# Linear attention and gated GLU: K features beside the Q projection, Q features beside the GLU stages, x turned by VectorE, output weights split in GLU 0

## The chip, the cores and the metric

The kernel runs on one core of one Trainium2 chip. The metric is the device time of one execution in microseconds; a version's time is the median of its runs. A profile is one execution, whose own time is given beside the time of the profiled span.

## What is computed

The input x is 2048 tokens of 1024 features, in fp32. After a layer norm it goes two ways, and the results are joined:

```python
xn = layernorm(x)
qkv = (xn @ wqkv)                      # q, k, v: 32 heads of 32
pq, pk = q @ w_phi, k @ w_phi          # per head
phi = concat(softmax(p), softmax(-p))  # 64 features, for q and k
kv, z = phi_k^T @ v, sum(phi_k)        # per head, over all tokens
s = (phi_q @ kv / (phi_q @ z + 1e-6)) @ wo
h = sigmoid(xn @ w_gate) * (xn @ w_up) # 3584 wide
out = x + s * silu(h @ w_down)
```

## The kernel before

All large products go to TensorE as f32r pairs: `split` (L121) casts a tile to f32r on ScalarE (L123) and has VectorE subtract that from the tile (L124), and `mm3` (L126) adds three matmuls, high by high, high by low, low by high. On top of that each large product is done with seven block products instead of eight; the blocks are named B11, T2, T3, B21, T1, T4 and B22. The T blocks and B22 of an operand are sums and differences of four quarters, made by GpSimd.

Tokens are done in two chunks of 1024 (`c` = 0, 1; eight tiles of 128 each). TensorE runs through six stages: the projections V, K, Q of chunk 0 (each seven blocks of four token tiles), GLU 0 (gate and up products of chunk 0: 28 units of seven blocks, twelve matmuls each), the same two for chunk 1, then down (`dsteps`), and the output stage (`attend` and wo). w_phi is folded into the K and Q weights, so that a projection's result is already the argument of the softmax.

Around these products stand tasks that other engines do:

- `k_task` (L429): loads k and v of a token tile and of one half of the heads (`hb`), takes the softmax features (`features`, L401: two reductions and two subtractions on VectorE, the exponential on ScalarE, a sum and a reciprocal on VectorE), scales them, splits features and v, adds them into `zacc`. Its small matmuls (`kv_products`, L454) come with the next task. There are 32, and after each 16 three finals (`kv_sum`, `kv_blocks`, `z_broadcast`).
- `q_features` (L565): the same features for q, kept in DRAM (`e_d`, `r_d`), for chunk 0 only. `q_task` (L573) in down loads them, or makes the features itself for chunk 1, then divides by the denominators and stores them into `f_d`.
- `x_task` (L501): loads a tile of chunk 1's x, norms it, turns it by eight TensorE transposes into PSUM (`transpose`, L183), copies it out on ScalarE and stores the block operands into `xo_d`. `load_operand` (L205) fetches them at the end of GLU 0 in two halves, through slots 53 and 54, and splits them into x0 to x6.
- `o_sums` (L256) and `wd_sums` (L546): the sums for wo's and w_down's blocks, into DRAM. `wo_prep` (L617) loads a piece of wo through a ring of two half slots and splits it, in down and at the turn into the output stage.

What sets the order: instructions are emitted in the order of the program, and a scheduler that simulates the engines places them; each engine then runs its own list in order. `background` (L768) takes the next task of a queue and lets it be issued after an anchor, an evacuation of the block at hand. Before, queue `bg` holds 16 q features and 8 x tasks, then K tasks and finals, and `bg2` the sums. GLU 0 takes one task per unit at T2 (L859), chunk 1's projections take the first eight K tasks (L793), GLU 1 a task every six blocks and a sum every ten (L862 to L866), and down the `q_task`s (L938). On-chip memory is cut into slots: 0 to 27 for the x operands, 28 to 35 for split weights (a ring of eight), 36 to 38 `p`, 39 to 42 `fa`, 43 to 46 `fb`, 47 to 54 `fc`. Loads and stores are issued by SyncE, in one list.

```python
            if c and len(bg) > 2 * (TT + 3) - EARLY and i not in (B11, B21):
                background(last_evac[0])
...
            if len(bg) > 2 * (TT + 3) and i == T2 and m > 7:
                background(v.ins)
```

## Time and profile before

| | us |
|---|---|
| median of three runs (lowest, highest) | 2428.53 (2424.84, 2431.23) |
| the profiled execution's own time | 2428.67 |
| its span | 2426.7 |
| TensorE busy in the span | 2364.4 |
| VectorE busy | 1752.7 |
| ScalarE busy | 999.1 |
| GpSimd busy | 982.7 |

The stages in the span lie at about 0 to 300 (chunk 0's projections), to 842 (GLU 0), to 1078 (chunk 1's projections), to 1654 (GLU 1), to 2207 (down) and to the end (output). PE is TensorE's matmuls, PEld its weight loads, DVE VectorE, ACT ScalarE, POOL GpSimd. A table by stretches gives the bounds of a stretch, its length, the busy time of the five with their instructions, the clock granted to TensorE as a share of full speed, the busy share of the DMA engines and GB/s. A row by line gives line, engine, operation, what it writes and reads, the shapes and the count, then busy time and the mean of one, then the idle time of its engine before it and what ended that. Matmul records overlap, so their lengths don't add up to time.

### The profile page before, as it was taken

To read this page: it belongs to the slowest core of one execution; us is meant where nothing else is said; L and a number is where in the kernel's file an instruction comes from. 1 tells how busy PE (TensorE), PEld (TensorE's weight loads), DVE (VectorE), ACT (ScalarE), POOL (GpSimd) and SP (SyncE) were. 2 spreads that over 40 slices of the span, in tenths; PEclk is the share of its full clock that TensorE was granted. 3 is DMA by queue.
4 is the path that set the end of the run, shared out by engine and by line. 5 is a ranking of instruction groups with operands and counts; after the bars stand their busy time and mean duration, and the time that the engine had idled before them with its cause. 6 is when DMAs were issued, how large, how long until landed. Compare 5 with 4: busy or idle time off the path is not lost.

```text
span 2426.7 us, 31652 instructions
## 1 busy us (share of the span) xinstructions
PE 2364.4 (97%) x10792; PEld 1957.0 (81%) x10792; DVE 1752.7 (72%) x2325; ACT 999.1 (41%) x1495; POOL 982.7 (40%) x638
## 2 busy tenths in 40 slices
PE   6999999999999999999999999999999999999998
PEld 5888888888888888888878888788888788877786
DVE  7533567777676688648858888746888998878775
ACT  6432244445444444324433444423443334355342
POOL 4530145665666410003454444442333344313555
PEclk9999999999999999999999999999999999999999
DMA  7874567777776764557888888796677767775564
GB/s 275 276 258 164 173 235 257 266 264 252 261 262 249 255 246 164 191 178 247 286 294 286 276 302 287 250 349 214 209 231 225 244 213 222 236 259 180 192 196 161
DMA packets 245329, 581.59 MB, mean 240 GB/s; under 512 B 31920, under 2 KB 48304, under 8 KB 240560
## 3 DMA queue, kind: packets, MB, share of 16 engines
q1 hardware_dynamic: 245168, 579.58, 69.8%
q8 instruction: 85, 1.39, 0.2%
q14 instruction: 76, 0.62, 0.1%
HBM read 353.76 MB, written 225.71 MB: 239 GB/s over the span
## 4 chain that ended last, share of the span: by engine, by line
PE 68%; DVE 10%; DMA 9%; issue 6%; POOL 4%; ACT 2%; SPq 1%; POOLq 0%; ACTq 0%; DVEq 0%
PE bank L128 22%; PE bank L129 22%; PE bank L130 22%; DVE x L124 2%; DVE w L124 2%; DMA fa<-w_down 1%; DMA w<-ws_d 1%; PE bank L454 1%; DMA fb<-w_down 1%; POOL fc L1020 1%; DMA fc<-wo 1%; DMA f_d<-fc 1%; POOL fc L1019 1%; DMA wf_d<-x 1%; ACT x L123 1%
## 5 line engine op out<-in xcount | busy, mean ns | idle before, releaser
L128 PE MATMUL bank<-x,w 128*128 128x512 f32 x2352 | 911.1, 391 | 9.5 <-DVE fb L835 2.9
L129 PE MATMUL bank<-x,w 128*128 128x512 f32 x2352 | 917.1, 390 | 2.3 <-DVE x L124 2.2
L130 PE MATMUL bank<-x,w 128*128 128x512 f32 x2352 | 904.5, 389 | 0.4 <-DVE w L124 0.4
L124 DVE TENSOR_TENSOR w<-fa,w 128x512 fp32r<-128x512 f32 (+1 forms) x444 | 436.7, 989 | 140.5 <-ACT w L123 139.0
L123 ACT CAST w<-fa 128x512 fp32r<-128x512 f32 (+1 forms) x444 | 307.9, 698 | 547.4 <-PE bank L129 337.5
L128 PEld LDWEIGHTS bank<-x,w 128*128 128x128 f32 x2352 | 441.3, 188 | 105.9 <-DVE fb L835 4.3
L129 PEld LDWEIGHTS bank<-x,w 128*128 128x128 f32 x2352 | 442.1, 188 | 95.0 <-DVE x L124 4.8
L130 PEld LDWEIGHTS bank<-x,w 128*128 128x128 f32 x2352 | 442.0, 188 | 92.5 <-DVE w L124 0.9
L128 PE MATMUL bank<-w,x 128*128 128x512 f32 x708 | 279.3, 395 | 8.0 <-ACT w L123 3.6
L130 PE MATMUL bank<-w,x 128*128 128x512 f32 x708 | 278.1, 394 | 6.1 <-DVE x L124 6.1
L129 PE MATMUL bank<-w,x 128*128 128x512 f32 x708 | 278.3, 393 | 0.0
L128 PEld LDWEIGHTS bank<-w,x 128*128 128x128 f32 x708 | 134.1, 189 | 38.3 <-ACT w L123 4.3
L843 POOL TENSOR_TENSOR fc<-fc 128x512 f32<-128x512 f32 x27 | 42.8, 1586 | 299.6 <-DVE fc L842 295.4
L130 PEld LDWEIGHTS bank<-w,x 128*128 128x128 f32 x708 | 134.3, 190 | 35.2 <-DVE x L124 7.7
L129 PEld LDWEIGHTS bank<-w,x 128*128 128x128 f32 x708 | 134.3, 190 | 27.1
L584 POOL TENSOR_TENSOR fc<-fc 128x1024 f32<-128x1024 f32 x32 | 81.0, 2530 | 181.2 <-ACT fc L419 122.0
L843 POOL TENSOR_TENSOR fb<-fb,fc 128x512 f32<-128x512 f32 x57 | 91.9, 1613 | 134.9 <-DVE fc L842 125.7
L317 POOL TENSOR_TENSOR fb<-fa 128x512 f32<-128x512 f32 x28 | 36.7, 1309 | 249.2 <-DMA fa<-w_gu 130.3
L124 DVE TENSOR_TENSOR w<-fb,w 128x512 fp32r<-128x512 f32 (+1 forms) x114 | 107.0, 939 | 30.7 <-ACT w L123 23.9
L123 ACT CAST w<-fb 128x512 fp32r<-128x512 f32 (+1 forms) x114 | 71.4, 626 | 135.4 <-PE bank L129 98.7
L842 DVE TENSOR_TENSOR fc<-fc,bank 128x512 f32<-128x512 f32 x84 | 57.2, 681 | 92.6 <-PE bank L130 77.4
L124 DVE TENSOR_TENSOR x<-fa,x 128x512 fp32r<-128x512 f32 x112 | 109.5, 979 | 18.0 <-ACT x L123 18.0
...
## 6 DMA issues: line engine op xcount, KB each, us to landing
ws_d<-w SPq DMA_DIRECT2D x112, 512.0 KB, 3.8
w<-ws_d SPq DMA_DIRECT2D x112, 512.0 KB, 5.6
fa<-w_gu SPq DMA_DIRECT2D x84, 512.0 KB, 4.2
fa<-h_d SPq DMA_DIRECT2D x84, 512.0 KB, 4.4
...
h_d<-fc SPq DMA_DIRECT2D x120, 256.0 KB, 3.6
...
```

The costliest lines, as they stand in the source:

```text
L123: nc.scalar.copy(o[0], src)
L124: return nc.vector.tensor_sub(o[1], src, o[0].bitcast(F32))
L128: nc.tensor.matmul(o, a[0], b[0], start=first, stop=False, **kw)
L129: nc.tensor.matmul(o, a[0], b[1], start=False, stop=False, **kw)
L130: nc.tensor.matmul(o, a[1], b[0], start=False, stop=last, **kw)
L317: nc.gpsimd.tensor_add(s1, a21, a22)
L454: nc.tensor.matmul(kvb[g // 2][:, g % 2 * 256:g % 2 * 256 + 256], v[:, g].rearrange("p a f -> p (a f)"), ph[:, g].rearrange("p a f -> p (a ...
L584: nc.gpsimd.tensor_mul(ez, e, zb)
L842: v = nc.vector.tensor_add(b, u2 if q == 3 else u1, bank)
L843: nc.gpsimd.tensor_mul(g, g, b)
L1019: eng.tensor_mul(y, y, g)
L1020: eng.tensor_add(y, y, xt)
```

## The change

- **x of chunk 1.** `x_task` becomes `x_fetch` and `x_turn`. The first norms the tile and stores it into `xs_d` in four pieces; the second loads it back rearranged and turns it with two VectorE transposes of 32x32 blocks, 128x512 each. Transposes on TensorE and copies on ScalarE are left for chunk 0 alone. The 1024 features stand in another order for this, so the host permutes the rows of the weights and chunk 0's x (`xk`) alike.
- **K.** The eight `k_task`s of chunk 0's first half of heads are queued in its Q projection (five blocks T2 to B22), and what is left of the queue in GLU 0. Chunk 1's projections take eight `wd_sums` at V and K, then five K tasks at Q. GLU 1 takes the other 19 with the finals.
- **q.** 16 `q_features` of chunk 0 stay in GLU 0; the 16 of chunk 1 go to GLU 1. `q_task` in down only loads them.
- **wo.** `o_task` loads, sums and splits a quarter of wo (seven splits) and stores the pairs into `wo_d`; four of them stand at the end of GLU 0's queue. `wo_prep` is one load.
- **Pace.** GLU 0 takes a task at T2 of each unit and also at T4 of the first 14. GLU 1 takes one every four blocks, from one queue in which K and finals, six `wd_sums` and 16 `q_features` are mixed evenly.

The diff, cut to its core:

```diff
...
@@ -182,17 +187,14 @@
-        c, th, u = t // CTT, t % CTT // 4, t % 4
+        th, u = t // 4, t % 4
         for q in range(2):
...
                 nc.tensor.transpose(tp[:, k * P:(k + 1) * P], xt[:, (4 * q + k) * P:(4 * q + k + 1) * P], ident)
-            i = {(0, 0): B11, (1, 0): B21, (1, 1): B22}.get((q, th))
-            if c == 0 and th == 0:
-                operand(c, i, u, tp)
+            if th == 0:
+                operand(0, (B11, B21)[q], u, tp)
             nc.scalar.copy(dst[q], tp)
-            if c and i is not None:
-                operand(c, i, u, dst[q])
...
@@ -253,10 +254,26 @@
-    def o_sums(k, bs):
+    def o_task(k):
+
+        def keep(i, b):
+            o = slots[o_r.next()]
+            split((o[:, 0].bitcast(F32R), o[:, 1].bitcast(F32R)), b)
+            nc.sync.dma_start(wo_d[i, k], o.bitcast(F32).rearrange("p a n -> p (a n)"))
+
+        a11, a12, a21, a22 = bs = halves(52, 53)
         for b, (f, h) in zip(bs, ((0, 0), (0, 1), (1, 0), (1, 1))):
             nc.sync.dma_start(b, wo[(k + 4 * h) * P:(k + 4 * h + 1) * P, f * HB:(f + 1) * HB])
-        w_sums(O, k, *bs)
+        for i, b in ((B11, a11), (B21, a12), (T4, a22)):
+            keep(i, b)
+        nc.gpsimd.tensor_add(a22, a21, a22)
+        nc.gpsimd.tensor_sub(a21, a11, a21)
+        nc.gpsimd.tensor_sub(a11, a22, a11)
+        nc.gpsimd.tensor_sub(a12, a12, a11)
+        for i, b in ((T2, a11), (T3, a21), (T1, a22), (B22, a12)):
+            keep(i, b)
+
+    o_r = Ring((36, 37, 38))
...
@@ -498,13 +519,26 @@
-    def x_task(t):
+    def x_fetch(t):
         xt = x_load(t, 52)
         norm([t], [xt])
+        for n in range(4):
+            nc.sync.dma_start(xs_d[t - CTT, :, :, n].rearrange("q s c -> s q c"),
+                              xt[n * DH:(n + 1) * DH].rearrange("s (q c) -> s q c", q=4))
+
+    def x_turn(t):
         th, u = t % CTT // 4, t % 4
-        transpose(t, xt, halves(53 + th))
+        dst = halves(53 + th)
+        xt = whole(52)
+        nc.sync.dma_start(xt, xs_d[t - CTT].rearrange("q s n c -> (q s) (n c)"))
+        for q in range(2):
+            nc.vector.transpose(dst[q].rearrange("p (k n s) -> p n k s", n=4, s=DH),
+                                xt.rearrange("p (n k d) -> p n k d", n=4, d=DH)[:, :, 4 * q:4 * q + 4])
+            i = {(0, 0): B11, (1, 0): B21, (1, 1): B22}.get((q, th))
+            if i is not None:
+                operand(1, i, u, dst[q])
         if th:
-            x_sums(t // CTT, u, halves(53), halves(54))
+            x_sums(1, u, halves(53), halves(54))
...
@@ -557,14 +591,14 @@
     eqr = Ring((50, 51))
-    qraw = Ring([slots[53][:, 1]])
     zb = whole(54)
-    qf_raw, qf_e = Ring(halves(36)), Ring((37, 38))
+    qf = Ring(((36, 0, 37), (36, 1, 38))), Ring(((43, 0, 44),))
...
-        p, e = qf_raw.next(), whole(qf_e.next())
+        r, a, e = qf[t // CTT].next()
+        p, e = slots[r][:, a], whole(e)
         nc.sync.dma_start(p, qkv_d[Q, t, hb])
...
@@ -572,14 +606,9 @@
         e, ez = whole(eqr.next()), whole(52)
-        if t < CTT:
-            nc.sync.dma_start(e, e_d[t, hb])
-            r = small.tile([P, 32], F32, name=f"r{t}{hb}", tag="r", bufs=2)
-            nc.sync.dma_start(r, r_d[t, hb])
-        else:
-            p = qraw.next()
-            nc.sync.dma_start(p, qkv_d[Q, t, hb])
-            r = features(f"q{t}{hb}", p, e, True)
+        nc.sync.dma_start(e, e_d[t, hb])
+        r = small.tile([P, 32], F32, name=f"r{t}{hb}", tag="r", bufs=2)
+        nc.sync.dma_start(r, r_d[t, hb])
         st = small.tile([P, 5, 16], F32, name=f"sa{t}{hb}", tag="sa", bufs=2)
...
@@ -615,13 +643,7 @@
     def wo_prep(i, k):
-        r = wor.next()
-        if i in (B11, B21, T4):
-            f, h = {B11: (0, 0), B21: (0, 1), T4: (1, 1)}[i]
-            nc.sync.dma_start(r, wo[(k + 4 * h) * P:(k + 4 * h + 1) * P, f * HB:(f + 1) * HB])
-        else:
-            nc.sync.dma_start(r, wf_d[O, i, :, k])
-        split(pair(WO[i][k]), r)
+        nc.sync.dma_start(slots[WO[i][k]].bitcast(F32).rearrange("p a n -> p (a n)"), wo_d[i, k])
...
@@ -753,22 +775,27 @@
-    bg, bg2 = deque(), deque()
-    for n, t in enumerate(CTT + 4 * a + q for q in range(4) for a in range(2)):
-        bg.extend([lambda n=n, hb=hb: q_features(n, hb) for hb in range(2)])
-        bg.append(lambda t=t: x_task(t))
+    ks = [[lambda t=t, hb=hb: k_task(hb, t) for t in range(TT)] for hb in range(2)]
     for hb in range(2):
-        bg.extend([lambda hb=hb, t=t: k_task(hb, t) for t in range(TT)])
-        bg.extend([lambda hb=hb, f=f: f(hb) for f in (kv_sum, kv_blocks, z_broadcast)])
-    bg2.extend([lambda k=k: o_sums(k, halves(43, 44)) for k in range(4)])
-    bg2.extend([lambda j=j: wd_sums(j, halves(43, 44)) for j in range(NJ)])
-    EARLY = 8
-    tick = [0, 0]
-
-    def background(anchor, tasks=None):
-        if tasks is None:
-            tasks = bg
-            kv_products()
+        ks[hb] += [lambda hb=hb, f=f: f(hb) for f in (kv_sum, kv_blocks, z_broadcast)]
+    qs = [lambda t=t, hb=hb: q_features(t, hb) for t in range(TT) for hb in range(2)]
+    wd = [lambda j=j: wd_sums(j, *((47, 52) if j < WD1 else (43, 44))) for j in range(NJ)]
+    xs = []
+    for q in range(4):
+        for a in range(2):
+            t = CTT + 4 * a + q
+            xs += [lambda t=t: x_fetch(t), lambda t=t: x_turn(t)]
+    bg_proj0 = deque(ks[0][:CTT])
+    bg_glu0 = deque([lambda: block("p", 36, 3, F32)])
+    for n in range(16):
+        bg_glu0.extend([xs[n], qs[n]])
+    bg_glu0.extend([lambda k=k: o_task(k) for k in range(4)])
+    bg_proj1 = deque(wd[:WD1])
+    late_k = deque(ks[0][CTT:] + ks[1])
+    bg_glu1 = deque()
+
+    def background(anchor, tasks):
+        kv_products()
         if tasks:
...
@@ -790,8 +817,12 @@
                 proj_out(c, what, i, u, pbank[u])
-            if c and len(bg) > 2 * (TT + 3) - EARLY and i not in (B11, B21):
-                background(last_evac[0])
+            if c == 0 and what == Q and i == B21:
+                block("p", 36, 3, F32R)
+            if c == 0 and what == Q and i not in (B11, B21):
+                background(last_evac[0], bg_proj0)
+            if c and not (what == V and i in (B11, B21)):
+                background(last_evac[0], bg_proj1 if bg_proj1 else late_k if what == Q and i not in (B11, B21) else ())
             continue
...
@@ -856,14 +887,17 @@
         if c == 0:
-            if len(bg) > 2 * (TT + 3) and i == T2 and m > 7:
-                background(v.ins)
+            if i == T2 and m > 7 or i == T4 and u < 14:
+                background(v.ins, bg_proj0 or bg_glu0)
         else:
-            if m >= 1 and (m - 1) % 6 == 0:
-                background(v.ins)
-            if m >= 10 and m % 10 == 0:
-                with tc.issue_after(last_load[0]):
-                    background(v.ins, bg2)
+            if m == 0:
+                rest = [deque(a) for a in (late_k, wd[WD1:], qs[16:])]
+                total = [len(a) for a in rest]
+                while any(rest):
+                    q = max(range(3), key=lambda q: len(rest[q]) / total[q])
+                    bg_glu1.append(rest[q].popleft())
+            if m and m % 4 == 0:
+                background(v.ins, bg_glu1)
         if c == 0 and u % (2 * NJ) == 2 * NJ - 1:
...
@@ -1028,13 +1064,15 @@
     f = lambda a: np.ascontiguousarray(np.asarray(a))
-    wqkv = np.asarray(A_wqkv)
-    gu = np.stack([np.asarray(B_w_gate), np.asarray(B_w_up)])
+    rows = np.arange(D).reshape(4, KT, DH).transpose(1, 0, 2).reshape(-1)
+    wqkv = np.asarray(A_wqkv)[rows]
+    gu = np.stack([np.asarray(B_w_gate)[rows], np.asarray(B_w_up)[rows]])
     gu = gu.reshape(2, KT, P, NF, P).transpose(3, 0, 2, 1, 4)
...
         "x": f(A_x).reshape(S, D),
+        "xk": f(np.asarray(A_x).reshape(S, D)[:CT, rows]),
         "wqkT": f(qk),
```

VectorE's list at the first units of GLU 0, before: L842 and L825 are evacuations of PSUM banks, L124 splits of weights, L408 to L422 one `q_features`.

```order
L842 TENSOR_TENSOR fc_94<-fc_94,bank_98 128x512
L124 TENSOR_TENSOR w_90<-fa_92,w_90 128x512
L124 TENSOR_TENSOR w_90<-fb_93,w_90 128x512
L825 TENSOR_TENSOR fc_94<-fc_94,bank_96 128x512
L408 TENSOR_REDUCE stq_2221<-p_91 128x16
L409 TENSOR_REDUCE stq_2221<-p_91 128x16
L417 TENSOR_TENSOR p_91<-p_91,stq_2221 128x2x256
L827 TENSOR_TENSOR fc_94<-fc_94,bank_97 128x512
L418 TENSOR_TENSOR p_91<-stq_2221,p_91 128x2x256
```

And after, at the same place (L129 is the split, L856 to L873 the evacuations; `stk` and L425 to L463 belong to K tasks):

```order
L856 TENSOR_TENSOR fc_97<-fc_97,bank_99 128x512
L129 TENSOR_TENSOR w_93<-fa_95,w_93 128x512
L438 TENSOR_REDUCE stk_1937<-fc_97 128x32
L129 TENSOR_TENSOR p_1613<-fc_97,p_1613 128x8x64
L425 TENSOR_REDUCE stk_2033<-fc_97 128x16
L426 TENSOR_REDUCE stk_2033<-fc_97 128x16
L439 RECIPROCAL stk_1937<-stk_1937 128x32
L129 TENSOR_TENSOR w_93<-fb_96,w_93 128x512
L452 TENSOR_TENSOR fc_97<-fc_97,stk_1937 128x1024
L858 TENSOR_TENSOR fc_97<-fc_97,bank_100 128x512
L129 TENSOR_TENSOR w_93<-fb_96,w_93 128x512
```

Instructions of two K tasks now stand between the evacuations and splits, where one q feature's stood.

ScalarE's list as TensorE goes from GLU 0 to chunk 1's V, before: L381 copies B11's four results, L123 casts x operands and weights.

```order
L123 CAST w_90<-fa_92 128x2x512
L381 COPY fc_94<-bank_95 128x512
L123 CAST x_0_86<-fc_94 128x4x256 x2
L123 CAST w_90<-fa_92 128x2x512
L381 COPY fc_94<-bank_96 128x512
L123 CAST x_0_83<-fc_94 128x4x256 x2
L381 COPY fc_94<-bank_97 128x512
L123 CAST w_90<-fa_92 128x2x512 x2
L381 COPY fc_94<-bank_98 128x512
```

After (L398 copies B11, L401 B21, L128 casts; `p` is the last `o_task`'s, `x_0_90` and `x_0_91` the first two operands' first halves):

```order
L398 COPY fc_97<-bank_101 128x512
L128 CAST x_0_89<-fc_97 128x4x256
L401 COPY fb_96<-bank_100 128x512
L401 COPY fb_96<-bank_101 128x512
L128 CAST p_2406<-fc_97 128x512 x3
L128 CAST x_0_86<-fc_97 128x4x256
L128 CAST p_2406<-fc_97 128x512
L128 CAST x_0_90<-fc_97 128x4x256
L128 CAST x_1_660<-fc_97 128x4x256
L128 CAST x_0_91<-fc_97 128x4x256
```

The first halves of B11's and B21's x now come after the copies of products that used the second halves, and after casts of wo.

SyncE's list there, before (`xo_d` into `fc` is `load_operand`, both halves of B11's in one row):

```order
L181 DMA xo_d<-fc_94 128x512 x4
L359 DMA ws_d<-w_90 128x1024
L181 DMA xo_d<-fc_94 128x512
L209 DMA fc_94<-xo_d 128x1024 x2
L359 DMA ws_d<-w_90 128x1024
```

And after, when those of the first two operands' first halves are issued (L262 stores wo's pairs, L561 loads w_down):

```order
L392 DMA qkv_d<-fb_96 128x512
L262 DMA wo_d<-p_2406 128x1024
L561 DMA fc_97<-w_down 128x512 x2
L262 DMA wo_d<-p_2406 128x1024 x2
L211 DMA fc_97<-xo_d 128x1024 x2
L262 DMA wo_d<-p_2406 128x1024
```

The two first halves stand together behind three stores of `p`, which wait for the casts above.

## Rows read from the trace of the kernel before

**Rows 1.** Busy us by stage: span, PE, PEld, DVE, ACT, POOL; clock, DMA.

```profile
300.00:842.00 542.00, 540.55 (x2414) 447.51 (x2413) 387.83 (x526) 244.85 (x362) 313.01 (x215) 1.00 0.71 256
842.00:1078.00 236.00, 236.00 (x1068) 196.48 (x1067) 164.50 (x194) 86.47 (x100) 11.20 (x6) 1.00 0.56 193
1078.00:1654.00 576.00, 565.68 (x2576) 468.42 (x2576) 425.13 (x510) 233.46 (x320) 254.44 (x171) 1.00 0.82 283
1654.00:2207.00 553.00, 546.33 (x2422) 448.82 (x2421) 473.04 (x685) 239.14 (x398) 191.84 (x93) 1.00 0.70 226
2207.00:2427.00 220.00, 199.06 (x990) 166.21 (x988) 154.57 (x215) 81.90 (x151) 119.67 (x84) 0.97 0.58 185
```

**Rows 2.** The same view, the first 120 us of GLU stage 0.

```profile
300.00:420.00 120.00, 120.00 (x536) 99.43 (x535) 84.43 (x113) 52.48 (x78) 63.01 (x45) 1.00 0.69 249
```

**Rows 3.** TensorE around a turn of x: start, length, what, idle before.

```profile
431.52 1.04 PE L189 MATMUL bank<-ident,fc 128*128 128x128 f32 x8
432.93 0.73 PE L128 MATMUL bank<-x,w 128*128 128x512 f32 x2 [0.36 <-ACT fb L833]
```

**Rows 4.** VectorE by line, 300 to 420: busy us, mean ns, idle before.

```profile
L124 DVE TENSOR_TENSOR w<-fb,w 128x512 fp32r<-128x512 f32 x26 | 26.0, 1001 | 6.8 <-ACT w L123 6.6
...
L842 DVE TENSOR_TENSOR fc<-fc,bank 128x512 f32<-128x512 f32 x9 | 6.1, 677 | 9.5 <-PE bank L130 9.5
```

**Rows 5.** The same, 420 to 842 us.

```profile
L417 DVE TENSOR_TENSOR p<-p,stq 128x512 f32<-128x512 f32 x12 | 18.0, 1504 | 0.0
...
L160 DVE BATCH_NORM_STATS2 bn<-fc 128x6 f32<-128x512 f32 x14 | 9.0, 681 | 0.0
...
L422 DVE RECIPROCAL stq<-stq 128x32 f32<-128x32 f32 x12 | 4.2, 347 | 0.2
...
L163 DVE TENSOR_SCALAR lnw<-mv 128x1 f32<-128x1 f32 x7 | 1.0, 144 | 0.0
```

**Rows 6.** The same, chunk 1's projections, 842 to 1078 us.

```profile
L124 DVE TENSOR_TENSOR p<-fc,p 128x1024 fp32r<-128x1024 f32 x8 | 9.7, 1218 | 0.3 <-ACT p L123 0.3
...
L422 DVE RECIPROCAL stk<-stk 128x32 f32<-128x32 f32 x8 | 2.8, 347 | 0.1
L124 DVE TENSOR_TENSOR w<-fa,w 128x512 fp32r<-128x512 f32 x3 | 2.1, 690 | 2.0 <-ACT w L123 2.0
```

**Rows 7.** The same, inside GLU stage 1, 1140 to 1560 us.

```profile
L124 DVE TENSOR_TENSOR p<-fc,p 128x1024 fp32r<-128x1024 f32 x21 | 34.3, 1632 | 0.0
...
L422 DVE RECIPROCAL stk<-stk 128x32 f32<-128x32 f32 x21 | 7.3, 346 | 0.1
```

**Rows 8.** VectorE's turns of 128x512 in the output stage.

```profile
L634 DVE STREAM_TRANSPOSE bank<-fc 128x512 f32<-128x512 f32 x64 | 45.7, 716 | 5.6 <-DMA fc<-f_d 5.1
```

**Rows 9.** ScalarE by line, chunk 1's projections, 842 to 1078 us.

```profile
L123 ACT CAST x<-fc 128x1024 fp32r<-128x1024 f32 x10 | 10.5, 1053 | 13.2 <-DMA fc<-xo_d 13.2
...
L384 ACT COPY fb<-bank 128x512 f32<-128x512 f32 x12 | 6.9, 583 | 6.8 <-PE bank L130 6.8
L123 ACT CAST p<-fc 128x512 fp32r<-128x512 f32 x7 | 4.3, 620 | 4.6 <-PE bank L454 4.6
```

**Rows 10.** DMA issues: KB each, median us from issue to landing.

```profile
fc<-xo_d SPq DMA_DIRECT2D x14, 512.0 KB, 4.7
```

**Rows 11.** What TensorE waited for, GLU stage 1: total us, times, longest.

```profile
PE bank L454 <- DVE p L124: 3.7, 4, 1.4
```

**Rows 12.** The same at the turn into the output stage, 2140 to 2280.

```profile
PE bank L128 <- ACT w L123: 3.6, 1, 3.6
PE bank L129 <- DVE x L124: 3.5, 6, 1.1
...
PE bank L128 <- ACT x L123: 0.2, 1, 0.2
```

**Rows 13.** Busy time and clock in the two slowest stretches of the turn.

```profile
2230.00:2240.00 10.00, 8.37 (x34) 6.68 (x35) 9.54 (x12) 6.49 (x14) 7.47 (x5) 0.83 0.73 223
...
2260.00:2270.00 10.00, 7.97 (x34) 6.67 (x35) 10.00 (x15) 5.75 (x11) 3.58 (x3) 0.72 0.29 86
```

35 lines of the change are left out of this document (22 added, 13 removed).

## The prediction

> **What bounds the kernel now.** I read the busy times by stage first [rows 1]: TensorE is busy 540.6 of 542 us in GLU 0, all of 236 in chunk 1's projections, 565.7 of 576 in GLU 1, 546.3 of 553 in down. There only fewer TensorE instructions or fewer waits shorten the time, and whatever VectorE is given must fit beside it. VectorE has room: 388 of 542 in GLU 0, 165 of 236 in chunk 1's projections, 425 of 576 in GLU 1, but 473 of 553 in down. TensorE's slack is in GLU 1 (10 us), down (7) and the output stage (21 of 220). The waits say who made it: the small kv products wait 3.7 us for VectorE's splits in GLU 1 [rows 11]; at the turn into the output stage it waits for wo's splits and those queued beside them, 3.6 us in one piece for a half on ScalarE, 3.5 in six for halves on VectorE [rows 12], and the clock falls, to a mean of 0.83 and 0.72 in two windows of 10 us [rows 13].
>
> **Part 1: x turned by VectorE.** 64 TensorE transposes leave GLU 0. A group of eight moves the next product from 431.52 to 432.93, 1.41 us, of which 0.36 is idle on ScalarE [rows 3]; without a wait it is 1.04 less the 0.16 by which records overlap, 0.88. There are eight groups, four with such a wait: 4 x 1.41 + 4 x 0.88 = **-9.2 us**, on the path, since TensorE is the bound there. VectorE gets 16 turns of 128x512. SBUF to SBUF is not in the trace; the turn into PSUM takes 0.716 [rows 8], so 1.43 a tile, and twice that is the upper bound. The round trip through DRAM is hidden by the 19 us of the unit that follows. With wo's and q's traffic GLU 0 moves 26 MB more in 542 us, 256 + 48 = 304 GB/s; GLU 1 ran at 283 with TensorE busy [rows 1], so I cost this at nothing, and it would show as late weights.
> For the transposes the trace decides: eight start to end in 1.04 us, 0.13 apiece [rows 3]. The Trainium skill ("TensorE: Matmul & The Clock Gate", Part 4: PE-mode transpose) gives about 275 ns each within a kernel; As a cost in sequence that would make the gain of 64 an estimated 17.6 us and the sum 8 lower; the measured 0.13 decides.
>
> **Part 2: K features of chunk 0 earlier.** The durations first. K's ten VectorE instructions, first and last of them in [rows 6] and [rows 7], sum to 8.6 us where GpSimd rests (chunk 1's projections) and 10.6 inside GLU 1 where it works. Six of q's, between the L417 and L422 rows, sum to 5.4 in GLU 0; the nine of a norm, L160 to L163, to 33.3/7 = 4.8 [rows 5]. A weight split takes 0.69 alone [rows 6] and 1.00 at GLU 0's start [rows 4]. Chunk 0's Q projection issues five K tasks, but in VectorE's order the instructions of five, two of these and the three issued later, stand in GLU 0's first units. Of the first 120 us there, VectorE works 84.4 [rows 2]. Take out four q features (21.5) and one norm (4.8): 58.1 are left. Put in five K (53.0), three q (16.1), two norms (9.5), two turns (2.9): 139.6 in 120, so 20 us too much. Each K also waits for its exponential on ScalarE, about as long as the cast of the same 1024 columns, 1.05 [rows 9], with the hand-over some 1.4: another 7 for five. Against it stands what VectorE may run late before TensorE feels it. Weights are split up to eight ahead (12 products of 0.226 each, 540.6 less 9 over 2352, so 22 us at most), but the evacuations stand in the same queue and free four banks, two or three of those steps: I take 7. **+20 us**, bounds 0 (all covered) and 33 (no cover, and 6 for a start that is late already). Nothing gives it back: in units 6 to 13 the task rate is doubled, and the same sum (303.4 busy in 422 us [rows 1, 2] less twelve q and seven norms, 206, gives 0.49 per us; plus eight q, four norms, four turns) is 142 of 152 us. From unit 14 one task a unit is left, about 70%, and wo's 28 splits fit in the last four.
> GLU 1 takes chunk 1's 16 q features from down (+86 us of VectorE) and gives five K's to the projections before it (-53): 458 of 576 instead of 425 [rows 1]. The finals, which wait most, still come last. I take **+5**, bounds -8 (the even pacing removes the kv waits [rows 11]) and +15.
>
> **Part 3: the seam into chunk 1's projections.** Here the orders shown with the change count. The first half of each x operand is loaded into slot 53, which was chunk 1's x before and is now also the last o_task's. On SyncE the two first-half loads stand behind three stores of wo; on ScalarE those three p casts stand behind the copies that evacuate TensorE's first products. TensorE has the second halves early: 48 products of 0.226, 10.9 us, for the token tiles 2 and 3 of B11 and B21, and then needs the first half. From the end of these: a copy 0.58, three casts 1.86, a split 0.69, the load 4.7, the cast of x 1.05 [rows 6, 9, 10]: 8.9 us. The second operand's first half shares slot 53, so it waits for the first one's split, 1.2 by a p of that size [rows 6]: 1.2 + 4.7 + 1.05 = 7.0 against the 5.4 us of 24 products, 1.6 more. After idle stretches of 3 us the clock fell elsewhere, 0.83 over 10 us being 1.7 us lost [rows 13]. That is 8.9 + 1.6 + 1.7: **+12 us**, bounds 5 (the casts are early, only load and cast remain) and 18 (a second slow load). Before, TensorE was busy for all of 236 us here. The rest of the stage stays TensorE's: VectorE loses three of eight K's there, and the eight wd_sums that come in are GpSimd's and SyncE's.
>
> **Part 4: wo and q off the end.** wo's 28 splits leave VectorE and ScalarE in down and the output stage, and with them the two-slot ring that feeds them; one 512 KB load stays for each. Of the 14.0 us that TensorE waits between 2140 and 2280 in seven rows, 11.9 stand in six of them behind L123 or L124 (the two largest and the last in [rows 12]); the fallen clock, 0.83 and 0.72 in two windows of 10 us, costs 1.7 + 2.8 = 4.5 [rows 13]. I take 16 of 16.4. Down had 7 us of slack [rows 1]; with 16 q features gone from VectorE, 86 us of its 473, I take 2. **-18 us**, bounds -12 (attention's own splits remain the last to come) and -22.
>
> **The sum**, on the profiled execution's 2428.7 us (0.1 above the median 2428.5): -9.2 +20 +12 +5 -18 = +9.8, so **2439 us**. 0.3% is 7.3 us, about what a measurement of this kernel can tell from no change: below 2421 is faster, above 2436 slower.
>
> **Rivals.** *Absorbed*: VectorE's surplus is hidden as in chunk 1's projections before, where eight K's in a row cost TensorE nothing in 236 us [rows 1]. For it: the ring of eight weights. Against it: there VectorE had 71 us of room in 236, here it is asked 140 in 120. With +1 in GLU 0, +8 at the seam and nothing in GLU 1: 2428.7 - 9.2 + 1 + 8 - 18 = 2410.5, and 2415 with the 5 of GLU 1; I take 2413. *Half absorbed*: +8 in GLU 0, the rest as forecast, 2427: no change. *Slower still*, and the other side of any gain: VectorE's two-input instructions and GpSimd's. A split of 0.69 becomes 1.00 in GLU 0 [rows 4, 6], while a sum with one input in PSUM keeps 0.68. GpSimd runs 215 instructions there [rows 1], 7.7 a unit. Where VectorE always has something queued, each may hold up a split's whole 0.69 instead of lengthening it by 0.31: 14 crowded units x 7.7 x 0.38 = 41 us, and less three tenths, for GpSimd work beside sums from PSUM and reductions, 29 on top: 2468. It decides from the point where VectorE has no idle left, which is what the first units are.
> The Trainium skill ("SBUF — State Buffer", Who interferes with whom) says that a VectorE instruction with two SBUF inputs contends with a GpSimd instruction that reads SBUF, and that issue order decides who blocks; the trace agrees, 1.00 against 0.69 [rows 4, 6]. By that rule GpSimd may as well be the one that waits, which would put the same microseconds on the gates instead.
> *It doesn't do what it says*: K's are issued beside the Q projection, yet run in GLU 0. That is in my forecast; were all eight done before GLU 0, it would be the first rival.
>
> **Chances.** Forecast 0.47 (2430 to 2452), absorbed 0.27, half absorbed 0.16, contention 0.10. Faster 0.26, same 0.26, slower 0.48 (forecast 0.38 of its 0.47, contention 0.10). The range reaches from 2408 to 2463 and leaves out the upper half of the contention case and the edges of the others.
>
> **What would show it.** Part 1: no L189 in GLU 0 for chunk 1 and no waits of its successor. Part 2: VectorE busy over 110 of the first 120 us of GLU 0, and TensorE waiting there for splits or evacuations; if TensorE's 300 to 842 stretch has the same length less 9, I am wrong and the time is near 2413. Part 3: one idle of TensorE of 7 to 13 us at the start of chunk 1's V, released by a cast of x. Part 4: no wait of 3 us and no clock below 1 between 2140 and 2280. A new wait at the end of GLU 1, where the finals come last, would put the time above the range.

## The result and the profile after

The changed kernel takes 2438.5 us in the median of six runs (2436.1 to 2441.8), the kernel before 2427.6 (2424.8 to 2431.2) beside it. The ratio is 1.0046, with a 95% interval of 1.0033 to 1.0059: slower by half a per cent, and half a us from the forecast of 2439. That the number was hit says little yet, so the terms come next. The profiled execution took 2439.9 us, its span is 2438.0, against 2428.7 and 2426.7.

The busy times by stage, which answer to [rows 1] (start and end, length, then busy us of PE, PEld, DVE, ACT, POOL with their instructions, the granted clock, the DMA share, GB/s):

```profile
302.00:866.00 564.00, 549.46 (x2401) 448.29 (x2400) 479.68 (x620) 268.65 (x392) 350.11 (x227) 0.99 0.83 294
866.00:1119.00 253.00, 233.95 (x1030) 192.85 (x1029) 136.31 (x152) 80.40 (x95) 63.05 (x42) 0.97 0.76 260
1119.00:1685.00 566.00, 560.79 (x2552) 466.09 (x2551) 448.67 (x577) 244.36 (x330) 184.28 (x123) 1.00 0.78 267
1685.00:2233.00 548.00, 543.62 (x2421) 449.27 (x2420) 407.58 (x571) 206.76 (x360) 197.12 (x95) 1.00 0.74 244
2233.00:2438.00 205.00, 193.76 (x991) 164.79 (x990) 147.30 (x203) 76.40 (x139) 118.31 (x84) 0.98 0.62 206
```

GLU 0 is 564 us long instead of 543, and VectorE works 480 us in it instead of 388. Chunk 1's projections are 252 instead of 235, and TensorE, busy for all of them before, is idle for 19 us there. GLU 1, down and the output stage are shorter by 10, 5 and 15 us.

To compare kernels I use one table. A stage runs from its first large product to that of the next. *Lost* is its length less its matmuls at the pace that undisturbed stretches show: 0.2265 us for 128x512, 0.1195 for 128x256, 0.110 for 128x128. It holds stalls and time at half clock alike, and is read from one execution of each kernel.

| kernel (profiled execution) | chunk 0 proj. | GLU 0 | chunk 1 proj. | GLU 1 | down | output | span |
|---|---|---|---|---|---|---|---|
| before: length | 288.4 | 542.9 | 235.3 | 576.4 | 553.0 | 219.6 | 2426.7 |
| before: lost | 25.8 | 3.1 | 0.3 | 16.2 | 12.0 | 29.8 | |
| after: length | 291.2 | 564.2 | 252.1 | 566.5 | 548.1 | 204.7 | 2438.0 |
| after: lost | 26.7 | 25.7 | 21.8 | 9.2 | 7.1 | 14.9 | |

The K tasks' small products (128x256, eight each) moved between the stages too: two K's to chunk 0's projections, six into GLU 0 (+5.7 us), five out of chunk 1's (-4.8), three out of GLU 1 (-2.9).

**GLU 0's start.** The first 120 us by engine, the answer to [rows 2]:

```profile
302.00:422.00 120.00, 108.00 (x463) 85.33 (x462) 109.81 (x138) 57.73 (x80) 56.38 (x34) 0.96 0.64 221
```

Four of VectorE's rows by line there (busy us, mean ns, idle before):

```profile
L129 DVE TENSOR_TENSOR w<-fb,w 128x512 fp32r<-128x512 f32 x20 | 19.8, 991 | 0.0
...
L452 DVE TENSOR_TENSOR fc<-fc,stk 128x1024 f32<-128x1024 f32 x6 | 8.3, 1388 | 0.0
...
L438 DVE TENSOR_REDUCE stk<-fc 128x32 f32<-128x1024 f32 x5 | 6.1, 1213 | 5.1 <-ACT fc L436 5.1
...
L425 DVE TENSOR_REDUCE stq<-p 128x16 f32<-128x512 f32 x2 | 1.4, 684 | 3.4 <-DMA p<-qkv_d 3.4
```

VectorE is busy 109.8 us where it was 84.4, and TensorE only 108.0 where it was 120. What TensorE waited for in GLU 0 (total, times, longest):

```profile
PE bank L133 <- DVE fc L858: 5.1, 6, 2.3
PE bank L133 <- DVE fc L873: 2.9, 1, 2.9
PE bank L133 <- ACT fc L854: 2.5, 3, 1.1
PE bank L475 <- DVE p L129: 1.9, 2, 1.0
```

The nine rows of that list, of which these are the largest four, sum to 14.6 of the 25.7 us lost, and all are evacuations of PSUM banks or K's splits; no wait is for a weight's split, so the ring of eight weights was cover enough and the four banks were not. The clock, 0.96 of full over the first 120 us, costs about 5 more; the other 6 are not attributed. Not all of it is work: at 402 to 407 us VectorE is not overloaded, it stands still. VectorE in order of time (start, length):

```profile
405.38 0.69 DVE L425 TENSOR_REDUCE stq<-p 128x16 f32<-128x512 f32 x1 [3.38 <-DMA p<-qkv_d]
...
406.58 0.68 DVE L873 TENSOR_TENSOR fc<-fc,bank 128x512 f32<-128x512 f32 x1
```

TensorE over the same stretch:

```profile
407.41 0.47 PE L133 MATMUL bank<-x,w 128*128 128x512 f32 x1 [2.88 <-DVE fc L873]
...
408.10 0.63 PE L135 MATMUL bank<-x,w 128*128 128x512 f32 x1
```

A q feature's first reduction waits 3.38 us for its load, the evacuation L873 stands behind it in VectorE's list, TensorE waits 2.88 us for that, and then its products are 0.63 long instead of 0.39, while the mean granted clock from 400 to 410 us is 0.89.

**The seam.** TensorE waits once for 18 us, by its list of waits:

```profile
PE bank L133 <- ACT x L128: 18.0, 1, 18.0
```

The busy times and the clock around it, in windows of 10 us:

```profile
880.00:890.00 10.00, 0.00 (x0) 0.00 (x0) 4.33 (x5) 3.32 (x5) 2.41 (x2) 0.61 0.95 338
890.00:900.00 10.00, 4.27 (x12) 3.39 (x13) 2.45 (x2) 2.09 (x2) 3.23 (x3) 0.54 0.87 290
900.00:910.00 10.00, 8.94 (x38) 6.78 (x37) 4.72 (x4) 5.45 (x7) 2.00 (x2) 1.00 0.88 265
```

The last pieces of the chain that ends it (start, length, what):

```profile
877.31 1.27 POOL fc L884
878.58 1.22 POOL fc L270
...
879.89 1.27 POOL fc L271
881.17 0.63 ACT p L128
881.83 1.23 DVE p L129
...
885.43 0.43 SPq L262
...
885.91 8.70 DMA fc<-xo_d
894.63 1.05 ACT x L128
```

TensorE's last product with the second halves starts at 877.35. Then come GpSimd's last sum of the last GLU unit and two sums of the last `o_task` (877.3 to 881.2), a cast and a split of wo, SyncE's issues of three stores and two loads of w_down (883.1 to 885.9, cut short above), and the load of the x half, 8.70 us long, before its cast.

**The turn.** The answer to [rows 12], the same stretch counted from the end of down:

```profile
PE bank L135 <- DVE fa L129: 1.9, 1, 1.9
PE bank L133 <- ACT x L128: 0.9, 1, 0.9
PE bank L134 <- DVE fb L129: 0.3, 1, 0.3
```

3.1 us are left of 14.0, and one window of 10 us with the clock under 0.9, at 0.83, where there were two.

**GLU 1.** TensorE's waits there before, beside the one of [rows 11] (L475 is a final's product here, the rest evacuations):

```profile
PE bank L128 <- DVE fb L835: 2.9, 2, 2.4
PE bank L128 <- ACT fc L833: 1.5, 1, 1.5
PE bank L475 <- POOL fb L532: 1.2, 1, 1.2
PE bank L128 <- ACT fb L833: 0.9, 1, 0.9
```

And all of them after (L475 now stands for K's products):

```profile
PE bank L133 <- ACT fb L864: 2.7, 1, 2.7
PE bank L475 <- DVE p L129: 1.8, 2, 1.0
PE bank L133 <- DVE fc L866: 0.7, 1, 0.7
```

10.2 us have become 5.2.

### The profile page after: what moved, and what is told of

Read it like the earlier page. It is cut to its first block, busy times and chain, and to the rows that moved or that the text cites. A ratio compares the mean times of both kernels' runs of the same rounds, so it can differ in the third digit from the quotient of the medians.

```text
span 2438.0 us, 31721 instructions
## 1 busy us (share of the span) xinstructions
PE 2360.2 (97%) x10728; PEld 1951.7 (80%) x10728; DVE 1786.3 (73%) x2341; ACT 996.5 (41%) x1485; POOL 1006.2 (41%) x638
## 4 chain that ended last, share of the span: by engine, by line
PE 68%; DVE 13%; DMA 8%; issue 5%; POOL 3%; ACT 2%; SPq 1%; POOLq 0%; DVEq 0%; ACTq 0%
PE bank L133 22%; PE bank L135 22%; PE bank L134 22%; DVE w L129 3%; DVE x L129 1%; DMA fa<-w_down 1%; DVE p L129 1%; PE bank L475 1%; DMA fc<-xo_d 1%; DVE fc L452 1%; DMA f_d<-fc 1%; DMA fc<-qkv_d 0%; POOL fb L874 0%; DVE fc L435 0%; DMA w<-ws_d 0%
## 5 line engine op out<-in xcount | busy, mean ns | idle before, releaser
L133 PE MATMUL bank<-x,w 128*128 128x512 f32 x2352 | 912.2, 391 | 19.3 <-DVE fc L858 5.1
L129 DVE TENSOR_TENSOR w<-fa,w 128x512 fp32r<-128x512 f32 (+1 forms) x444 | 447.7, 1012 | 213.5 <-ACT w L128 208.6
L128 ACT CAST w<-fa 128x512 fp32r<-128x512 f32 (+1 forms) x444 | 308.4, 698 | 532.7 <-PE bank L134 385.9
L133 PE MATMUL bank<-w,x 128*128 128x512 f32 x708 | 279.5, 396 | 22.2 <-ACT x L128 19.8
L874 POOL TENSOR_TENSOR fb<-fb,fc 128x512 f32<-128x512 f32 x57 | 90.5, 1588 | 219.5 <-DVE fc L873 202.7
L133 PEld LDWEIGHTS bank<-w,x 128*128 128x128 f32 x708 | 134.6, 190 | 52.2 <-ACT x L128 21.5
L134 PEld LDWEIGHTS bank<-w,x 128*128 128x128 f32 x708 | 134.6, 190 | 26.7
L129 DVE TENSOR_TENSOR x<-fa,x 128x512 fp32r<-128x512 f32 x112 | 117.1, 1046 | 33.8 <-ACT x L128 33.8
L129 DVE TENSOR_TENSOR w<-fb,w 128x512 fp32r<-128x512 f32 (+1 forms) x114 | 116.2, 1020 | 14.7 <-ACT w L128 14.6
L128 ACT CAST p<-fc 128x512 fp32r<-128x512 f32 x100 | 74.9, 756 | 124.6 <-DVE fc L452 77.8
L129 DVE TENSOR_TENSOR p<-fc,p 128x512 fp32r<-128x512 f32 x100 | 112.0, 1127 | 16.8 <-ACT p L128 16.7
L128 ACT CAST w<-fb 128x512 fp32r<-128x512 f32 (+1 forms) x114 | 70.7, 623 | 85.1 <-PE bank L134 70.7
```

The source lines that it names most:

```text
L128: nc.scalar.copy(o[0], src)
L129: return nc.vector.tensor_sub(o[1], src, o[0].bitcast(F32))
L133: nc.tensor.matmul(o, a[0], b[0], start=first, stop=False, **kw)
L134: nc.tensor.matmul(o, a[0], b[1], start=False, stop=False, **kw)
L874: nc.gpsimd.tensor_mul(g, g, b)
```

## The experiments

Three questions were open: what makes the idle at the seam, what makes the loss in GLU 0, and whether the other terms are right or only cancel. All kernels are the changed one with the edit shown, unless said otherwise; times are medians, and each is compared with runs of the kernel before on the same chip (2430.5, 2427.7 and 2428.4 us in the three sets, 2427.6 beside the changed kernel). Where two kernels of different sets are compared, the ratios are the safer measure, and the text gives both where they differ.

The table gives stage lengths of the profiled executions, with what is lost in brackets where the text uses it. Each is one execution, whose own time stands beside the median. Where a stage's own tasks are the same, executions still differ: GLU 0 lost 24.3 to 27.3 us in five kernels (the changed one, wo in chunk 1's proj., slot 38, wo split late, q in down), chunk 1's projections 1.7 to 8.7 in three (slot 38, its even pace, q in down), and GLU 1 took 566 to 572 in five (the changed one, three K's out, slot 38, its even pace, K first). Smaller differences between two rows show nothing.

| kernel | median us | profiled execution us | ratio to before (95%) | GLU 0 | chunk 1 proj. | GLU 1 | down | output |
|---|---|---|---|---|---|---|---|---|
| wo in chunk 1's proj. | 2429.2 | 2429.4 | 0.9994 (0.9982 to 1.0005) | 562.8 (24.3) | 233.7 (5.4) | 575.2 (15.9) | 551.2 | 202.1 |
| three K's out | 2417.4 | 2417.1 | 0.9946 (0.9931 to 0.9961) | 554.4 (18.8) | 239.5 (6.5) | 566.3 (8.9) | 551.8 | 201.2 |
| both out | 2437.6 | 2446.9 | 1.0030 (1.0014 to 1.0045) | 553.1 (17.6) | 241.3 (12.9) | 592.9 (30.7) | 551.2 | 204.3 |
| slot 38 | 2424.5 | 2424.1 | 0.9975 (0.9963 to 0.9987) | 562.8 (24.3) | 236.8 (6.5) | 567.0 (9.7) | 550.0 | 203.4 |
| slot 38, even pace | 2425.9 | 2432.7 | 0.9998 (0.9984 to 1.0011) | 561.4 (22.9) | 238.9 (8.7) | 572.1 (14.7) | 552.9 | 202.6 |
| slot 38, even pace, three K's out | 2414.5 | 2418.0 | 0.9950 (0.9936 to 0.9964) | 542.1 (6.5) | 237.5 (6.3) | 576.9 (17.6) | 553.3 | 203.7 |
| the same, K first | 2415.1 | 2410.0 | 0.9956 (0.9940 to 0.9973) | 542.9 (7.3) | 243.3 (10.2) | 568.0 (10.7) | 549.5 | 202.7 |
| the same, six w_down sums | 2409.1 | 2410.7 | 0.9921 (0.9904 to 0.9939) | 543.1 (7.5) | 236.6 (3.5) | 573.0 (15.7) | 551.2 | 202.6 |
| before, x turn in one task | 2439.2 | 2437.8 | 1.0050 (1.0035 to 1.0065) | 552.0 (19.3) | 235.3 (0.3) | 577.1 | 554.1 | 217.9 |
| before, x turn in two tasks | 2418.8 | 2420.6 | 0.9961 (0.9947 to 0.9976) | 533.1 (0.4) | 235.3 (0.3) | 574.6 | 554.8 | 219.0 |
| slot 38, wo split late | 2428.1 | 2432.4 | 0.9997 (0.9986 to 1.0009) | 564.8 | 230.4 (0.2) | 568.2 | 551.2 | 210.2 (20.1) |
| slot 38, q in down | 2421.0 | 2418.7 | 0.9970 (0.9959 to 0.9981) | 565.8 | 231.9 (1.7) | 565.5 (8.2) | 551.1 | 200.4 (10.6) |

### The seam: wo elsewhere, and another slot

```diff
-    bg_glu0.extend([lambda k=k: o_task(k) for k in range(4)])
-    bg_proj1 = deque(wd[:WD1])
+    bg_proj1 = deque(wd[:WD1] + [lambda k=k: o_task(k) for k in range(4)])
```

> The changed kernel with the four wo tasks moved from the end of GLU 0 to the last four K blocks of chunk 1's projections; nothing else. Theory (the 18 us idle at the seam is the wait of the first operands' first halves for slot 53, held by the last wo task, with its GpSimd sums, casts and stores ahead of the load): the idle goes to under 2 us and the clock stays whole there, 20 us less than the changed kernel's 2438.5, about 2418; GLU 0 keeps its 25 us of lost time. Rival (the loads are late because GLU 0's end moves 357 GB/s, or because the x chain itself ends late): more than 8 us of the idle stay, 2430 or more.

The idle is gone: 5.4 us are lost in chunk 1's projections instead of 21.8, and GLU 0 is as before the edit, 24.3 lost. But the time fell by 9 us (13 by the ratios), not 20. GLU 1 is 575.2 instead of 566.5: the K tasks behind the wo tasks slip into it.

The finer cut leaves every task at its place and takes another slot for half of wo's input:

```diff
-        a11, a12, a21, a22 = bs = halves(52, 53)
+        a11, a12, a21, a22 = bs = halves(52, 38)
...
-    o_r = Ring((36, 37, 38))
+    o_r = Ring((36, 37))
```

> The changed kernel with one slot exchanged: the wo tasks take slots 52 and 38 instead of 52 and 53, and their results a ring of two slots instead of three. Casts, sums, stores and their place in the program stay. Theory (slot 53 is what the x halves wait for): the seam's idle goes to under 3 us, total about 2420. Rival (casts, GpSimd sums and stores in the same queues delay the x loads whatever the slot): 8 us or more stay, 2430 or more.

2424.5 us, 14 less (17 by the ratios). Casts, sums and stores of wo are all still there, and TensorE's only wait in the seam is this:

```profile
PE bank L133 <- DVE fc L873: 1.1, 1, 1.1
```

So slot 53 makes the idle, as the first theory says; casts, sums and stores alone don't. With the slot the loads also got free of their place behind wo's stores, for six of the 14 are now issued by 868.3 us, where the changed kernel had issued three; the run doesn't part the two. Nor are the loads faster here (from issue to landing, least, median and longest, of all 14 x halves, after the edit):

```profile
DMA to landing us min/median/max: 4.3/6.3/10.1
```

### GLU 0: the K tasks or the pace

```diff
...
-        if (hb, t) == (0, CTT):
+        if (hb, t) == (0, 5):
             nc.sync.dma_start(zacc, zk_d)
...
-    bg_proj0 = deque(ks[0][:CTT])
+    bg_proj0 = deque(ks[0][:5])
...
-    bg_proj1 = deque(wd[:WD1])
+    bg_proj1 = deque(wd[:WD1] + ks[0][5:CTT])
```

> The changed kernel with three of the eight early K tasks taken out of GLU 0 and done at the K blocks of chunk 1's projections; five stay queued at chunk 0's Q. Theory (VectorE is asked for 140 us in GLU 0's first 120): 32 us leave it, so TensorE's lost time in GLU 0 falls from 25.7 to about 8, the seam stays at 18, total about 2421. Rival (the doubled pace of x and q tasks, or the traffic of 330 GB/s, makes the loss): 20 us or more stay lost, 2433 or more.

The total is near what was expected, 2417.4 for 2421, and its reasons are not. GLU 0 loses 18.8 instead of 25.7, 7 less and not 17, and gives up three K's small products. The seam, which I expected to stay, went: with three tasks fewer in GLU 0's queue the wo tasks come three units earlier and have freed slot 53 in time. That agrees with the slot's part, but it was not in the expectation.

```diff
-            if i == T2 and m > 7 or i == T4 and u < 14:
+            if i == T2 and m > 7 or i == T4 and u % 2 == 0:
```

> The changed kernel with wo's tasks in slots 52 and 38 (as in the run before it with that exchange, 2424.5 us, 24.3 lost in GLU 0), and one thing more: GLU 0's 14 extra task places at T4 lie at every second unit instead of at each of the first 14. The three K tasks and all others stay. Theory (the doubled pace keeps VectorE at 108 of 120 us after the K's, so it can't catch up, and makes about half of the loss): lost time in GLU 0 falls to about 14, total about 2414. Rival (the K tasks alone make the loss): 21 or more stay, 2421 or more.

Only 1.4 us less are lost, about what two executions differ by, and the total is no better (0.9998 of the kernel before, where slot 38 alone has 0.9975). By this run the pace alone is not the cause; by the one before, the K's alone are the smaller part. Both edits together, with 11 places for the pace because three tasks fewer are queued:

```diff
-            if i == T2 and m > 7 or i == T4 and u < 14:
+            if i == T2 and m > 7 or i == T4 and u % 2 == 0 and 0 < u < 24:
```

> Slots 52 and 38 for wo, three K tasks done in chunk 1's projections, and the 11 extra places that GLU 0 then needs at every second unit from 2 to 22. Theory: of the 18.8 us lost in GLU 0 with the three K's out, the pace made ten; about 8 stay, the K's carried over from chunk 0's Q. Total about 2407. Rival (the five K's carried over from Q make the rest): 16 or more stay, 2414 or more.

6.5 us are lost in GLU 0, though three K's of chunk 0's Q still have their products there; the rival falls. So one edit takes 1, the other 7 and both take 18 of 24. I read this as a backlog on VectorE, which drains only when what comes in falls under what VectorE can do. VectorE's own waits agree: in the first 120 us it waited 25.4 us for products of TensorE before the change ([rows 4] show 9.5 of them), and none in the changed kernel, with the three K's out or with the even pace; with both it waits 7.9 us again. The first 120 us by engine with the three K's out:

```profile
302.00:422.00 120.00, 114.29 (x505) 92.14 (x504) 108.82 (x149) 63.89 (x88) 63.55 (x41) 1.00 0.81 283
```

And with the even pace as well:

```profile
302.00:422.00 120.00, 117.00 (x522) 95.71 (x521) 101.46 (x139) 61.79 (x87) 59.81 (x39) 1.00 0.75 265
```

108.8 us against 101.5 of VectorE, 114.3 against 117.0 of TensorE. The gain did not arrive in the total: the median is 2414.5, 10 less than with slot 38 alone (6 by the ratios), and by the ratios no less than with the three K's out alone (0.9950 and 0.9946). GLU 0 is 12 us shorter than there, and GLU 1 11 us longer, 577 instead of 566.

### Where the backlog goes instead

```diff
...
-    bg_proj0 = deque(ks[0][:CTT])
+    bg_proj0 = deque(ks[0][:5])
...
-    bg_glu0.extend([lambda k=k: o_task(k) for k in range(4)])
-    bg_proj1 = deque(wd[:WD1])
+    bg_proj1 = deque(wd[:WD1] + [lambda k=k: o_task(k) for k in range(4)] + ks[0][5:CTT])
```

> Both edits at once: wo's tasks and three K tasks in chunk 1's projections, five K tasks at chunk 0's Q. Theory (the two losses are independent): 2438.5 - 20 - 17, about 2401, faster than the kernel before by about 1%; VectorE in chunk 1's projections about 175 of 236 us, TensorE loses under 3 there. Rival (chunk 1's projections now lose what GLU 0 gave back, or GLU 1 does): 2415 or more.

My theory of two independent losses is wrong here. The median is that of the changed kernel (4 us less by the ratios). The profiled execution is the slowest of ten, 9 us over the median (they spread from 2428.5 to 2446.9), so its stages say where the loss lies rather than how large it is. In it GLU 0 and chunk 1's projections are 11 us shorter each, and GLU 1 is 26 us longer: five K's more than in the changed kernel now have their products in it (216 small products against 176, 4.8 us by themselves); that the rest is work which chunk 1's projections left behind is argued, not shown. In those, one stall is 8.8 us long, by TensorE's waits:

```profile
PE bank L133 <- DVE fb L395: 8.8, 1, 8.8
```

The chain through it is wo's again (start, length, what):

```profile
987.36 4.12 DMA wd_d<-fc
...
991.49 3.20 DMA fc<-wo
...
994.71 0.63 ACT p L128
...
995.37 0.70 DVE p L129
```

A load of wo waits for the stores of a w_down sum, for both use slot 52; the split of wo waits for the load; and VectorE, idle for 13 us ahead of that split, has an evacuation behind it.

Two further edits tested this sharing. In the first, the three K's stand before the w_down sums:

```diff
...
-    bg_proj1 = deque(wd[:WD1])
+    bg_proj1 = deque(ks[0][5:CTT] + wd[:WD1])
```

> As the run with the even pace and three K tasks out, but in chunk 1's projections these three K tasks come before the eight w_down sums instead of after them, at the first three blocks of V that take a task. Theory (late K tasks leave a backlog on VectorE that the Q projection's five K tasks and GLU 1 pay for; early ones are worked off): the stall of 4.5 us at the K projection goes, 4 to 6 us less than that run, about 2402. Rival (the place in the stage doesn't matter): within 2 us of it.

No change in the median, as the rival said. But the place does matter: where the run before had two stalls of 2.1 and 2.2 us behind its last sum, this one has a single stall of 6.9 us, at the next place where a sum is followed by a K. VectorE stands idle for 12.5 us ahead of the split of that K's v, whose load into slot 52 was issued behind the sum's four stores. In the second, the sums are fewer and a place is left empty behind them:

```diff
-    WD1 = 8
+    WD1 = 6
...
-    bg_proj1 = deque(wd[:WD1])
+    bg_proj1 = deque(wd[:WD1] + [lambda: None] + ks[0][5:CTT])
...
-            if m and m % 4 == 0:
+            if m and (m % 4 == 0 or m in (30, 62, 94, 126)):
```

> As the run with the even pace and three K tasks out (2414.5 us), but chunk 1's projections take six w_down sums, then leave one place empty, then the three K's; GLU 1 takes the two sums more. Theory (w_down sums and K's share slot 52, and the K's loads wait for the last sum's stores while VectorE stands in order): no stall over 1 us in chunk 1's projections and 4 to 8 us less, about 2408. Rival (VectorE's work there, not the slot): within 2 us of it.

The median is 5.4 us less (7 by the ratios), as the theory asked. TensorE's waits in the stage are now these:

```profile
PE bank L133 <- DVE fb L395: 2.6, 2, 1.4
```

Two stalls of 1.2 and 1.4 us stay where none over 1 was expected, so the sharing is not all. Nor is it shown to be the whole gain: 3.5 us are lost in the stage instead of 6.3, two K's products moved from GLU 1 into it, and GLU 1, with two sums and four places more, is 3.9 us shorter. This is the fastest version that was run, 2409.1 us, 0.8% under the kernel before.

### x turned by VectorE, alone

On the kernel before, with fetch and turn in the task that had the TensorE transposes:

```diff
     def x_task(t):
         xt = x_load(t, 52)
         norm([t], [xt])
-        transpose(t, xt, halves(53 + th))
+        for n in range(4):
+            nc.sync.dma_start(xs_d[t - CTT, :, :, n].rearrange("q s c -> s q c"),
+                              xt[n * DH:(n + 1) * DH].rearrange("s (q c) -> s q c", q=4))
+        nc.sync.dma_start(xt, xs_d[t - CTT].rearrange("q s n c -> (q s) (n c)"))
+        for q in range(2):
+            nc.vector.transpose(dst[q].rearrange("p (k n s) -> p n k s", n=4, s=DH), ...)
...
```

> The kernel before with only the first part of the change: chunk 1's x goes through DRAM and is turned by two VectorE transposes a tile, in the same eight tasks. Theory (64 TensorE transposes leave a stage bound by TensorE, and VectorE has room there): 9 us less than before, GLU 0 at 534 us. Rival (VectorE's turns and the round trip cost as much by late weights or operands): within 3 us of before.

12 us slower. GLU 0 loses 19.3 us where it lost 3.1. The same kernel with the fetch beside a tile's first q feature and the turn two units later:

```diff
-        bg.extend([lambda n=n, hb=hb: q_features(n, hb) for hb in range(2)])
-        bg.append(lambda t=t: x_task(t))
+        bg.append(lambda n=n, t=t: (x_fetch(t), q_features(n, 0)))
+        bg.append(lambda n=n: q_features(n, 1))
+        bg.append(lambda t=t: x_turn(t))
```

> The kernel before with the x turn alone once more, now as the change has it: the fetch with the first of a tile's two q tasks, the turn two units later. As one task it was 12 us slower than before, with stalls of 2 to 3 us at VectorE's T3 evacuations. Theory (those came from how one long task falls into VectorE's list, not from the turn): without them the 9 us of 64 transposes show, about 2419. Rival (turn and round trip cost VectorE and the queues more than they free on TensorE at this place): 2430 or more, TensorE loses 12 us or more in GLU 0.

2418.8 us, 9.6 less than before, and GLU 0 has nothing left to lose. What differs is in VectorE's rows, here of the one task (idle before, and its releaser):

```profile
L839 DVE TENSOR_TENSOR fc<-fc,bank 128x512 f32<-128x512 f32 x22 | 14.7, 670 | 0.2
...
L513 DVE STREAM_TRANSPOSE fc<-fc 128x512 f32<-128x512 f32 x14 | 9.1, 691 | 34.4 <-DMA fc<-xs_d 34.4
```

And the turn's row of the two tasks:

```profile
L516 DVE STREAM_TRANSPOSE fc<-fc 128x512 f32<-128x512 f32 x14 | 9.1, 684 | 0.0
```

The turns themselves take 0.69 and 0.68 us. In the one task VectorE stands for 34.4 us before 14 of them, until the round trip through DRAM has landed, and the evacuations L839 behind it are what TensorE waits for:

```profile
PE bank L130 <- DVE fc L839: 10.4, 7, 2.8
```

### wo and q at the end

```diff
...
     def wo_prep(i, k):
-        nc.sync.dma_start(slots[WO[i][k]].bitcast(F32).rearrange("p a n -> p (a n)"), wo_d[i, k])
+        r = wor.next()
+        if i in (B11, B21, T4):
+            f, h = {B11: (0, 0), B21: (0, 1), T4: (1, 1)}[i]
+            nc.sync.dma_start(r, wo[(k + 4 * h) * P:(k + 4 * h + 1) * P, f * HB:(f + 1) * HB])
+        else:
+            nc.sync.dma_start(r, wf_d[O, i, :, k])
+        split(pair(WO[i][k]), r)
```

> The changed kernel with slots 52 and 38 for wo (2424.5 us as such), and wo's splits put back: the tasks in GLU 0 only make the sums, and down and the output stage load and split each piece through a ring of two half slots as before. Theory (the 28 splits and their ring were the waits at the turn): 16 us come back, nearly all between down's last products and the first attention products, total about 2440. Rival (q's features leaving down made that gain): under 5 us come back, 2429 or less.

Between the two theories: the output stage takes 210.2 us instead of 203.4, so 7 come back there and not 16. Chunk 1's projections are 6 us shorter, but not shown to be so for want of the splits: the next kernel has them and loses 1.7 us there. The counterpart keeps wo split early and puts chunk 1's q features back into down:

```diff
...
-        nc.sync.dma_start(e, e_d[t, hb])
+        if t < CTT:
+            nc.sync.dma_start(e, e_d[t, hb])
...
+        else:
+            p = qraw.next()
+            nc.sync.dma_start(p, qkv_d[Q, t, hb])
+            r = features(f"q{t}{hb}", p, e, True)
...
-                rest = [deque(a) for a in (late_k, wd[WD1:], qs[16:])]
+                rest = [deque(a) for a in (late_k, wd[WD1:])]
...
```

> The changed kernel with slots 52 and 38 for wo (2424.5 us), and chunk 1's 16 q features put back into down; GLU 1 then paces its tasks every six blocks. By the prediction's terms (q costs GLU 1 5 us, frees 2 in down): about 3 less, 2421. Rival, as the trace after suggests (GLU 1 took the q's at no cost, down gained about 5): 5 more, 2430.

The median is that of the prediction's terms, 3.5 us less, but by the ratios it is 1 us, within the noise, and the stages don't bear the terms out: GLU 1 differs by 1.5 us and down by 1.1. The run excludes the rival and says three things. Without 16 q's in it, and with VectorE at 387 us of work instead of 450, GLU 1 is as long as with them (its pace differs, too). With them in down, down is as short as without. And wo split early is enough by itself: the output stage takes 200.4 us.

Against 219.6 before, early wo alone brings 19 us in the output stage, q out of down alone (the run above) 9, and both 15 in the changed kernel and 15 to 18 in the other eight that have both. They don't add up; I take it that either one relieves the same queues on VectorE and ScalarE, which no run shows by itself.

## The prediction, step by step

| term | forecast us | measured us |
|---|---|---|
| GLU 0: x turned by VectorE | -9.2 | -9.8 (alone, as two tasks) |
| GLU 0: VectorE's surplus | +20 | +24.7 lost (1.0 to 25.7, the transposes' 2.1 of waits apart) |
| seam and chunk 1's projections | +12 | +21.5 lost |
| GLU 1 | +5 | -7.0 lost |
| down and output | -18 | -4.9 and -14.9 |
| chunk 0's projections | 0 | +0.9 lost |

The measured terms, with -9.1 for the transposes, sum to 11.2, and K's small products moved without a sum. So the time was right by luck, because terms were wrong in opposite senses: GLU 0 and the seam cost 14 us more than forecast, GLU 1 12 us less. The seam's 21.5 us lie outside the bounds given for it, 5 to 18; the other terms that were given bounds lie inside them.

**Part 1 holds**, in a form that the forecast named only in passing. "The round trip through DRAM is hidden by the 19 us of the unit that follows" is the step that decides: in one task the same 16 turns made the kernel 12 us slower, because the wait then stands in VectorE's list ahead of evacuations. A turn took 0.69 us, a little under the 0.716 that was taken from PSUM, and not the double that was the upper bound.

**Part 2's GLU 0** was right in direction and size, 24.7 for 20, within its bounds. Its picture of VectorE's sum was right enough: 139.6 us were asked of 120, 109.8 were done, a hair under the 110 named as its sign, and TensorE fell back by 12. That the doubled pace gives nothing back until unit 14 agrees with the runs, since neither edit alone removed the loss. What the sum missed are waits in the list, as at 402 us, where a load and not work held the evacuation, and half clock after them.

**The seam** failed by its size, and by two rows that were not in the chain. The forecast went from TensorE's last product to a copy, three casts, a split, a load of 4.7 us and a cast, 8.9 us. The chain shows 3.6 us of GpSimd first, because the last `o_task`'s sums stand behind the last GLU unit's; then 4.7 for a cast, a split and SyncE's issues where I had 3.1; then a load of 8.7 instead of the median 4.7 of [rows 10], issued behind 512 KB stores. That is 18.0 with the cast. The place, the slot and the releaser were as forecast.

**GLU 1** failed by its step, though its -7.0 lies within the bounds, -8 and +15. I weighed 16 q's and five K's by their VectorE time, +86 and -53. For the q's that was wrong: 63 us of VectorE's work more or less in GLU 1 went with 567.0 and 565.5 us. No row of TensorE's waits names a q, since nothing on TensorE reads one in this stage, while K's splits feed products that stand in TensorE's own list. What made the 7 us stays open. Of the 5.0 us by which the waits fell, 3.1 are those of K's products and finals and 1.9 those of evacuations. With products of 22 K's in the stage GLU 1 takes 565 to 573 us (seven kernels and the changed one), with 24 it takes 575 and 577, with 25 (before, and the two with the x turn alone) 575 to 577, with 27 it takes 593. That points to the K's; but three K's are 2.9 us by their products alone, the kernels with 25 have another pace and no q's, and no run changed the number of K's by itself. The even mixing, which the forecast named for its lower bound, wasn't tested apart either.

**Part 4** held: -19.8 for -18, the waits at the turn 3.1 of 14.0, the longest 1.9; but one window with the clock at 0.83 stayed, where the forecast wanted none below 1. Its attribution to wo holds as well; that q's leaving would have brought half of it alone was not seen.

Of the rivals, *absorbed* (+1 in GLU 0) and *half absorbed* (+8) fell with the 24.7 us there, and with them "eight K's in a row cost TensorE nothing": that was so where GpSimd rested and VectorE had room. The contention case, 29 us more, did not come: weight splits take 1.00 and 1.04 us in GLU 0 after, against the 1.00 of [rows 4].
